# Moving one pair's query exponentials behind the next pair's copies, and loading the next block's activations two steps ahead

## The chip, the cores and the metric

The kernel runs on one core of one Trainium2 chip. The metric is the time on the device in microseconds (us), where lower is better. The profiler's trace of one execution gives what each engine did: TensorE (PE, with its weight loads as PEld), VectorE (DVE), ScalarE (ACT), GpSimd (POOL), and SyncE (SP), which issues most DMAs here.

## The reference

Two things stand one behind the other: attention with a random feature map in place of a softmax, for 8 batches of 8 heads, 576 positions and head size 64, and then a gated layer over its output as 4608 tokens of 512 channels.

```python
def phi(x):
    proj = np.einsum('bhsd,df->bhsf', x, w_phi)          # 64 -> 128 features
    proj = proj - np.max(np.abs(proj), axis=-1, keepdims=True)
    return np.concatenate([np.exp(proj), np.exp(-proj)], axis=-1)
q_p, k_p = phi(q), phi(k)
kv = np.einsum('bhsf,bhsd->bhfd', k_p, v)
z = np.sum(k_p, axis=2)
num = np.einsum('bhsf,bhfd->bhsd', q_p, kv)
den = np.einsum('bhsf,bhf->bhs', q_p, z)[..., None] + 1e-06
attn = num / den
x = attn.transpose(0, 2, 1, 3).reshape(B * S, H * D)      # 4608 x 512
out = (x @ w_a) * (x @ w_b) @ w_out                       # 512 -> 1536 -> 512
```

## The kernel before, in words

**Attention.** The heads are worked on in 32 pairs, named by batch and pair (3_1 is the second pair of batch 3; the trace leaves the numbers out). `attention_steps` writes a plan: each pair is given a period of four turns, and each part of its work (project, kv_products, num_products and so on) a turn counted from the start of its period. Parts of neighbouring pairs therefore interleave. `project` is the part that the change touches. TensorE projects the first half of q (pq), then k (pk), then the second half of q (pq), each into one of a few PSUM buffers. ScalarE copies the two halves of q out into p (L199 and L211), VectorE takes k's largest absolute value (m, L178) and subtracts it (d, L179), and ScalarE makes the two exponentials e of k (L181, L182). In every second pair the last 64 positions of two pairs' k, the rest, are treated in the same way as e_r. The features of q lie across the partitions, so for q the largest absolute value is a reduction over partitions on GpSimd (mb, L217, two per pair), VectorE subtracts it from p (L218) and ScalarE makes q's two exponentials eq (L219, L220). Then e and v are multiplied (kv), the sums are put beside them, back copies the result out (L263), it is transposed (pt), copied to kvh (L271), and multiplied with eq into the numerator (pn, copied to x at L284) and the denominator (pd, copied to dn at L295). The denominator goes through memory: stored as den, loaded as r, inverted, stored as rec, loaded for all partitions as rb, multiplied into x, and x is stored as xnorm.

**The gated layer, first pass.** The first half of the layer's 1536 columns is done in blocks of 384 tokens. Pairs 0 to 9 run alone, for some 117 us. From then on `run` gives TensorE parts of `moe_block` between the parts of a pair. A block loads x in four chunks of 128 channels (`x_chunk`, tile x32 with two buffers), splits each into a rounded high part xh and a low part xl (`x_make`: ScalarE casts, VectorE subtracts, L143 and L144), then goes through six steps f, each with the products pa and pb, their product h, and its parts hh and hl, and then through four output chunks po, each copied to o (L583, two buffers) and stored as part (L584). Chunks 0 and 1 of the next block are issued at f = 2. Chunks 2 and 3 are issued in the output loop, each behind the split that gives its x32 buffer free. The weights w come in a packed form, and `load_weights` decodes them beside the first 200 us: ScalarE at L421, VectorE at L422 and L424, ScalarE's cast at L427, VectorE at L429, L430 and L433.

**What comes behind.** From about 540 to 660 us the factors of the second pass are made from its weights on VectorE and ScalarE beside the last blocks. The second pass, from about 777 us on, does the other half of the columns. The change leaves both as they are.

**What sets the order.** On TensorE the order of the attention's products and the blocks' products is the order in which the plan issues them, held by explicit dependences (`pe`). On ScalarE, VectorE and SyncE a scheduler sorts the instructions by what they wait for; `tc.issue_after(x)` keeps an instruction behind x. Each engine runs its instructions in that order.

Of the kernel before, what the change touches and what calls it, by code (L numbers as in the profile page):

```python
# [9 lines left out]
F32 = mybir.dt.float32  # L10
# [8 lines left out]
P = 128  # L19
# [25 lines left out]
def tile_kernel(ctx, tc, qP, km, kr, vm, vr, w_phi, eye, w_a, w_b, w_out, out):  # L45
# [139 lines left out]
    def project(b, pr, a1, a2, consts, st):  # L185

        w2 = consts[0]
        u = f"{b}_{pr}"
        k32, q32 = st["k", b, pr], st["q", b, pr]
        p32 = a2.tile([P, 2, S], F32, tag="p32", name=f"p32_{u}")  # L190

        def q_half(t):
            x = duo(f"pq_{u}_{t}")
            for j in range(2):
                mm(x[:, j, :HALF], w2[heads[j]], q32[heads[j], times[t]])
            return x

        x = q_half(0)
        nc.scalar.copy(p32[:, :, times[0]], x[:, :, :HALF])  # L199
        y = duo(f"pk_{u}")  # L200
        for c in range(NFULL):
            for j in range(2):
                mm(y[:, j, c * P : (c + 1) * P], k32[heads[j], c * P : (c + 1) * P], w2[heads[j]])
        i = b * NPAIR + pr
        place = alone["early"] if i <= ALONE and i % 2 else a1
        st["e", b, pr] = features(u, y, NFULL, place, a1, a2)
        x = q_half(1)
        if pr % 2 == 0:
            for j in range(2):
                mm(x[:, j, HALF : HALF + F], st["rk", b, pr // 2][heads[j]], w2[heads[j]])  # L210
        nc.scalar.copy(p32[:, :, times[1]], x[:, :, :HALF])  # L211
        if pr % 2 == 0:
            st["er", b, pr // 2] = features(f"r_{u}", x[:, :, HALF:], 1, a1, a1, a2)
        eq = a1.tile([P, 2, 2, S], F32, tag="eq", bufs=2, name=f"eq_{u}")
        for j in range(2):
            mb = a2.tile([P, S], F32, tag="mb", name=f"mb_{u}_{j}")
            nc.gpsimd.partition_all_reduce(mb, p32[:, j], P, bass_isa.ReduceOp.absmax)  # L217
            nc.vector.tensor_tensor(p32[:, j], p32[:, j], mb, op=ALU.subtract)  # L218
        nc.scalar.activation(eq[:, :, 0], p32, AF.Exp)  # L219
        nc.scalar.activation(eq[:, :, 1], p32, AF.Exp, scale=-1.0)  # L220
        st["eq", b, pr] = eq

    def summed(b, pr, a1, a2, consts, st):

# [101 lines left out]
    def attention_steps(pools, consts, st):  # L326
# [11 lines left out]
        for i in range(B * NPAIR):  # L338
            b, pr = divmod(i, NPAIR)
            t0 = TURNS * i  # L340
            args = (b, pr, *pools, consts, st)
            at = SPREAD if i < ALONE else PACKED
            if i == ALONE - 1:
                at = dict(SPREAD, turned_kv=8, num_products=8, den_products=8)
            elif i == ALONE:
                at = dict(PACKED, kv_products=4, z_products=4, kv_out=4)
            units = ((project, 0), (turned_kv, 0), (summed, 0), (kv_products, 0), (num_products, 0), (z_products, 0), (kv_out, 0))
            units += ((den_products, 0), (load_kq, -5), (load_v, -2 if i else 0))
            for order, (f, t) in enumerate(units):
                if f is not summed or i >= SUM_FROM:  # L350
                    plan(order, once(f, *args), [t0 + at.get(f.__name__, t)])
            rec_turns = REC_TURNS0 if i < ALONE - 4 else REC_TURNS1 if i < ALONE - 2 else REC_TURNS
            done = t0 + at["den_products"]
            plan(10, reciprocals(b, pr, *pools, st), [done + t for t in rec_turns])
            if b == 0:
                plan(11, x_first, [done + rec_turns[-1] + t for t in X_TURNS])
            if pr == NPAIR - 1:
                plan(12, b, [done + rec_turns[-1]])
# [131 lines left out]
        key, i = two[q, nm, k]  # L490
        return weights[key][:, i]

    def x_chunk(p, j, c, pool, bufs):

        T, u = TS[p], f"{p}_{j}"
        x32 = pool.tile([P, T], F32, tag="x32", bufs=bufs, name=f"x32_{u}_{c}")
        t = j * T
        while t < (j + 1) * T:
            b, s0 = divmod(t, S)
# [5 lines left out]
    def x_make(p, j, c, x32, pool):  # L505
        hl = [pool.tile([P, TS[p]], F32R, tag=f"x{k}", bufs=NCC, name=f"x{k}_{p}_{j}_{c}") for k in "hl"]
        split(*hl, x32, nc.scalar, nc.vector)
        block_x.setdefault(j, []).append(hl)

    def first_block_x():  # L510

# [8 lines left out]
    def moe_block(p, j):  # L520
# [17 lines left out]
        for f in range(NFS[p]):  # L538
# [18 lines left out]
            hs.append((hh, hl))  # L557
            if f == 2 and j + 1 < blocks[0]:
                loaded = [x_chunk(p, j + 1, c, pool, 2) for c in range(2)]
            yield  # L560
        dst = part.rearrange("(c p) s -> p c s", p=P)[:, :, j * T : (j + 1) * T]
        accs = {}
# [10 lines left out]
        for cc in range(ahead):  # L573
            outputs(cc, range(NFS[p] - 1))
        for cc in range(NCC):
            if loaded:
                x_make(p, j + 1, cc, loaded.pop(0), pool)
                if cc + 2 < NCC:
                    loaded.append(x_chunk(p, j + 1, cc + 2, pool, 2))
            outputs(cc, range(NFS[p] - 1 if cc < ahead else 0, NFS[p]))  # L580
            acc = accs[cc]
            o = hpool.tile([P, T], F32, tag="o", bufs=2, name=f"o_{p}_{j}_{cc}")
# [288 lines left out]
        return wpool, f"w_{f}_{nm}"  # L871

    kept, begun, feeds = {}, set(), []
    weights, pools_moe, xpools, block_x, blocks, marks, acts, loads, alone = {}, [], [xpool], {}, [0], [], [], [], dict(turn=0)
    begin = TURNS * (ALONE + 1)
    with ExitStack() as c:
        pools = attention_pools(c)
# [163 lines left out]
```

## Time and profile before

| what | value |
|---|---|
| median of 3 runs | 1190.28 us (1188.46 to 1190.87) |
| time of the profiled execution | 1188.66 us |
| its span | 1186.9 us |
| TensorE busy | 1143.6 us, 96% |
| VectorE busy | 753.6 us, 63% |
| ScalarE busy | 566.4 us, 48% |
| GpSimd busy | 141.8 us, 12% |
| granted TensorE clock, mean | 0.996 of full speed |

The time of an execution is its span and some 1.8 us round it. Busy times are summed over an engine's instructions. The span has stages with different limits, so a share of 96% says how much idle time there is, not where it lies: the tables by window and the waits tell that.

### The profile page before, as it was taken

The page shows a single profiled execution, that of the slowest core. Times are in us where ns is not written, and L with a number is a line of the kernel's source. Part 1 is how long each engine was busy: PE and PEld are TensorE (multiplying, and loading weights), DVE is VectorE, ACT ScalarE, POOL GpSimd, SP SyncE. Part 2 cuts the span into 40 slices and gives each one's busy share as a digit, 9 for nine tenths or more (in the row PEclk, how much of TensorE's full clock was granted, in tenths as well). Part 3 has the DMA queues.
Part 4 walks back from the last instruction along what each step waited for, and adds up shares of the span by engine and source line. Part 5 has one row for each costly group of instructions (what it writes and reads, how often), then busy time and mean ns, then how long its engine had stood idle before and what let it go on. Part 6 is the DMA issues. An engine that isn't in the chain of part 4 may idle for free.

```text
span 1186.9 us, 21022 instructions
## 1 busy us (share of the span) xinstructions
PE 1143.6 (96%) x8198; PEld 1028.5 (87%) x8198; DVE 753.6 (63%) x1359; ACT 566.4 (48%) x1050; POOL 141.8 (12%) x69
## 2 busy tenths in 40 slices
PE   8998898999999999999999999999999999999998
PEld 5665775878788788889899999999999999999997
DVE  6897876554555455543899222648577685958665
ACT  6886565554454455442555222435344353535332
POOL 4443322212121121210000000000000000000000
PEclk9999998999999999999999999999999999999999
DMA  6576554323232333214885111067685777768572
GB/s 210 161 216 202 173 159 124 111 78 115 82 121 88 104 95 94 88 33 146 292 308 200 54 54 40 20 201 273 191 303 173 259 223 233 245 206 281 173 250 84
DMA packets 103077, 191.76 MB, mean 162 GB/s; under 512 B 19521, under 2 KB 54721, under 8 KB 102977
## 3 DMA queue, kind: packets, MB, share of 16 engines
q1 hardware_dynamic: 102672, 190.28, 50.2%
q8 instruction: 65, 1.06, 0.4%
q14 instruction: 36, 0.29, 0.1%
q10 hardware_dynamic: 304, 0.13, 0.0%
HBM read 150.75 MB, written 39.62 MB: 160 GB/s over the span
## 4 chain that ended last, share of the span: by engine, by line
PE 72%; DVE 12%; DMA 9%; ACT 4%; issue 2%; SPq 1%; ACTq 0%; DVEq 0%
PE po L105 10%; PE pa L105 10%; PE po L772 10%; PE pb L105 10%; PE pa L661 9%; PE pb L661 9%; PE kv L105 5%; PE pn L105 4%; DMA x<-xnorm 3%; PE pq L105 2%; PE pd L105 2%; DMA back_w<-kept_w 1%; PE pk L105 1%; DVE m L178 1%; DMA rb<-rec 1%
## 5 line engine op out<-in xcount | busy, mean ns | idle before, releaser
L217 POOL PARTITION_ALL_REDUCE mb<-p x64 | 141.5, 2255 | 371.4 <-ACT p L211 316.7
L105 PE MATMUL pa<-xh,w_a 128*128 128x384 f32 x576 | 161.4, 341 | 0.0
L105 PE MATMUL pb<-xh,w_b 128*128 128x384 f32 x576 | 158.6, 336 | 0.7 <-ACT o L583 0.7
L105 PE MATMUL po<-hh,w_o 128*128 128x384 f32 x576 | 155.4, 343 | 2.2 <-ACT o L583 2.2
L105 PEld LDWEIGHTS po<-hh,w_o 128*128 128x128 f32 x576 | 105.8, 190 | 8.1 <-ACT o L583 2.8
L105 PEld LDWEIGHTS pa<-xh,w_a 128*128 128x128 f32 x576 | 105.1, 188 | 5.5 <-ACT back L263 2.8
L105 PEld LDWEIGHTS pb<-xh,w_b 128*128 128x128 f32 x576 | 105.1, 188 | 1.0 <-ACT o L583 1.0
L553 DVE TENSOR_TENSOR h<-pb,h 128x384 f32<-128x384 f32 x72 | 39.8, 552 | 94.5 <-PE pb L105 89.9
L105 PE MATMUL po<-hl,w_o 128*128 128x384 f32 x288 | 97.5, 339 | 1.1 <-DVE hl L144 1.1
L105 PE MATMUL pb<-xl,w_b 128*128 128x384 f32 x288 | 96.8, 336 | 0.0
L105 PE MATMUL pa<-xl,w_a 128*128 128x384 f32 x288 | 96.7, 336 | 0.0
L178 DVE TENSOR_REDUCE m<-pk 128x8 f32<-128x1024 f32 x32 | 39.1, 1220 | 83.5 <-PE pk L105 83.5
L143 ACT CAST hh<-h 128x384 fp32r<-128x384 f32 x72 | 37.0, 514 | 95.8 <-DVE h L553 95.7
L772 PE MATMUL po<-hh_s,own_o 128*128 128x384 f32 x288 | 80.3, 336 | 0.3 <-ACT u L760 0.3
L105 PE MATMUL pn<-eq,kvh 128*64 128x288 f32 x512 | 68.0, 408 | 8.5 <-DVE kvh L271 8.2
L105 PEld LDWEIGHTS pn<-eq,kvh 128*64 128x64 f32 x512 | 37.6, 137 | 33.3 <-ACT p L211 4.3
L105 PE MATMUL kv<-e,v 128*64 128x256 f32 x512 | 62.3, 385 | 0.9 <-ACT e L182 0.9
L772 PE MATMUL po<-hh_w,own_o 128*128 128x384 f32 x216 | 59.1, 334 | 0.0
L105 PE MATMUL pq<-q,w 64*128 64x288 f32 x256 | 49.3, 452 | 9.7 <-ACT p L199 9.7
L105 PEld LDWEIGHTS po<-hl,w_o 128*128 128x128 f32 x288 | 54.7, 190 | 1.4 <-DVE hl L144 1.4
L583 ACT COPY o<-po 128x384 f32<-128x384 f32 x48 | 22.5, 478 | 69.6 <-PE po L105 57.3
L105 PEld LDWEIGHTS pa<-xl,w_a 128*128 128x128 f32 x288 | 54.2, 188 | 0.0
(257 smaller groups left out, 2619.7 us busy)
## 6 DMA issues: line engine op xcount, KB each, us to landing
back_s<-kept_s SPq DMA_DIRECT2D x71, 512.0 KB
back_w<-kept_w SPq DMA_DIRECT2D x52, 512.0 KB
q<-in_qP SPq DMA_DIRECT2D x32, 288.0 KB
rb<-rec SPq DMA_DIRECT2D x64, 144.0 KB
xnorm<-x SPq DMA_DIRECT2D x32, 288.0 KB
part<-o SPq DMA_DIRECT2D x48, 192.0 KB
o<-part SPq DMA_DIRECT2D x24, 384.0 KB
out_x<-o SPq DMA_DIRECT2D x48, 192.0 KB
```

Of the source, the lines that this page charges most:

```text
L105: issue = lambda: nc.tensor.matmul(out, w, x, start=start, stop=stop, skip_group_check=True)
L143: (eng_hi.copy if eng_hi is nc.scalar else eng_hi.tensor_copy)(hi, src)
L178: nc.vector.tensor_reduce(out=m, in_=p, op=ALU.max, axis=AX.X, apply_absolute_value=True)
L217: nc.gpsimd.partition_all_reduce(mb, p32[:, j], P, bass_isa.ReduceOp.absmax)
L553: nc.vector.tensor_tensor(h32, pab["b"], h32, op=ALU.mult)
L583: nc.scalar.copy(o, acc)
L661: in_turn(lambda: nc.tensor.matmul(acc[to][i], w_, x_, skip_group_check=True, **at), u.startswith("1_0"))
L772: in_turn(lambda: nc.tensor.matmul(acc[m, to], w_, h_, skip_group_check=True, **f), False)
```

## The change

Two things are moved. First, q's exponentials have a part of their own in the plan, `q_features`, one period (four turns) behind `project`, and are kept behind the latest copy of a second half of q, which is then that of the next pair. Second, a block loads chunks 2 and 3 of the next block's x at f = 3, into the two buffers of tile o, and splits them first, in front of the first output chunk; chunks 0 and 1, still loaded at f = 2, are split in front of the second. `block_x` becomes a dictionary so that the chunks are found by number.

```diff
-        nc.scalar.copy(p32[:, :, times[1]], x[:, :, :HALF])
+        copies.append(nc.scalar.copy(p32[:, :, times[1]], x[:, :, :HALF]))
...
-        eq = a1.tile([P, 2, 2, S], F32, tag="eq", bufs=2, name=f"eq_{u}")
         for j in range(2):
             mb = a2.tile([P, S], F32, tag="mb", name=f"mb_{u}_{j}")
             nc.gpsimd.partition_all_reduce(mb, p32[:, j], P, bass_isa.ReduceOp.absmax)
             nc.vector.tensor_tensor(p32[:, j], p32[:, j], mb, op=ALU.subtract)
-        nc.scalar.activation(eq[:, :, 0], p32, AF.Exp)
-        nc.scalar.activation(eq[:, :, 1], p32, AF.Exp, scale=-1.0)
-        st["eq", b, pr] = eq
+        st["p", b, pr] = p32
+
+    def q_features(b, pr, a1, a2, consts, st):
+        eq = st["eq", b, pr] = a1.tile([P, 2, 2, S], F32, tag="eq", bufs=2, name=f"eq_{b}_{pr}")
+        with tc.issue_after(copies[-1].ins):
+            nc.scalar.activation(eq[:, :, 0], st["p", b, pr], AF.Exp)
+            nc.scalar.activation(eq[:, :, 1], st["p", b, pr], AF.Exp, scale=-1.0)
...
-            units = ((project, 0), (turned_kv, 0), ...
+            units = ((project, 0), (q_features, TURNS), (turned_kv, 0), ...
...
             if f == 2 and j + 1 < blocks[0]:
                 loaded = [x_chunk(p, j + 1, c, pool, 2) for c in range(2)]
+            if f == 3 and loaded:
+                loaded += [x_chunk(p, j + 1, c, hpool, 2, "o") for c in range(2, NCC)]
...
         for cc in range(NCC):
-            if loaded:
-                x_make(p, j + 1, cc, loaded.pop(0), pool)
-                if cc + 2 < NCC:
-                    loaded.append(x_chunk(p, j + 1, cc + 2, pool, 2))
+            if loaded and cc < 2:
+                for c in (2, 3) if cc == 0 else (0, 1):
+                    x_make(p, j + 1, c, loaded[c], pool)
```

On ScalarE, beside block 0, where pair 3_1 is projected, the order was this; the number behind a name tells tiles apart, 3_1 is the pair in p, and in eq, e and dn only the pair within its batch is named.

```order
L421 ACTIVATE w_1_o<-raw_1_o 128x512
L219 ACTIVATE eq_0_1760<-p_3_0_1726 128x2x576
L220 ACTIVATE eq_0_1760<-p_3_0_1726 128x2x576
L263 COPY back_0_1882<-kv_0_1840 128x384
L427 CAST w_1_o<-w_1_o 128x512
L295 ACTIVATE dn_3_1893<-pd_3_1884,eps 128x288
L199 COPY p_3_1_1913<-pq_1_0_1914 128x2x288
L211 COPY p_3_1_1913<-pq_1_1_1934 128x2x288
L181 ACTIVATE e_1_1931<-d_1_1927 128x8x128
L182 ACTIVATE e_1_1931<-d_1_1927 128x8x128
```

The changed kernel has the same work there in this order (its lines are numbered 3 higher from L216 on).

```order
L424 ACTIVATE w_1_o<-raw_1_o 128x512
L266 COPY back_0_1879<-kv_0_1837 128x384
L430 CAST w_1_o<-w_1_o 128x512
L298 ACTIVATE dn_3_1890<-pd_3_1881,eps 128x288
L199 COPY p_3_1_1910<-pq_1_0_1911 128x2x288
L211 COPY p_3_1_1910<-pq_1_1_1931 128x2x288
L223 ACTIVATE eq_0_1941<-p_3_0_1723 128x2x576
L224 ACTIVATE eq_0_1941<-p_3_0_1723 128x2x576
L181 ACTIVATE e_1_1928<-d_1_1924 128x8x128
L182 ACTIVATE e_1_1928<-d_1_1924 128x8x128
```

The exponentials eq of pair 3_0 have moved from in front of the copies of pair 3_1 to behind them, and now stand between the copies and the exponentials e of 3_1's k; the cast and dn still stand ahead of the first copy.

On ScalarE at the end of block 0, where pair 3_3 is projected, the order was this; xh_1_0 to xh_1_3 are the high parts of the chunks of block 1's x, and x_3_1 is the attention's numerator.

```order
L143 CAST xh_1_2_2498<-x_0_1_2_2357 128x384
L284 COPY x_3_1_2244<-pn_1_2235 128x576
L219 ACTIVATE eq_2_2148<-p_3_2_2114 128x2x576
L220 ACTIVATE eq_2_2148<-p_3_2_2114 128x2x576
L143 CAST xh_1_3_2532<-x_0_1_3_2425 128x384
L263 COPY back_2_2266<-kv_2_2224 128x384
L421 ACTIVATE w_5_o<-raw_5_o 128x512
L295 ACTIVATE dn_1_2277<-pd_1_2268,eps 128x288
L199 COPY p_3_3_2290<-pq_3_0_2291 128x2x288
L427 CAST w_5_o<-w_5_o 128x512
```

In the changed kernel the same stretch, with two rows more at either end, reads as follows.

```order
L143 CAST xh_1_3_2360<-x_0_1_3_1989 128x384
...
L430 CAST w_4_o<-w_4_o 128x512
L287 COPY x_3_1_2247<-pn_1_2238 128x576
L266 COPY back_2_2269<-kv_2_2227 128x384
L424 ACTIVATE w_5_o<-raw_5_o 128x512
L298 ACTIVATE dn_1_2280<-pd_1_2271,eps 128x288
L199 COPY p_3_3_2293<-pq_3_0_2294 128x2x288
L430 CAST w_5_o<-w_5_o 128x512
L211 COPY p_3_3_2293<-pq_3_1_2314 128x2x288
L223 ACTIVATE eq_2_2324<-p_3_2_2117 128x2x576
L224 ACTIVATE eq_2_2324<-p_3_2_2117 128x2x576
```

All of xh has moved ahead of the cast of w_4_o, so between that cast and q's copy only x's copy, back, the first step of w_5_o and dn are left.

On SyncE the loads of chunks 2 and 3 of block 1's x stood here, among the stores and loads of the denominators (rec, rb, den); xnorm_84 and xnorm_85 are batches 0 and 1 of the normalised x.

```order
L314 DMA rec_79<-r_0_2160 128x9
L501 DMA x_0_1_2_2357<-xnorm_84 128x192
L318 DMA rb_0_2324<-rec_79 64x576 x2
L501 DMA x_0_1_2_2357<-xnorm_85 128x192
L169 DMA v_4_0_2373<-in_vm 128x512
L501 DMA x_0_1_3_2425<-xnorm_84 128x192
L501 DMA x_0_1_3_2425<-xnorm_85 128x192
```

In the changed kernel they stand some 50 rows sooner, beside the loads of chunk 1.

```order
L321 DMA rb_3_1580<-rec_77 64x576 x2
L504 DMA x_0_1_2_1986<-xnorm_84 128x192
L504 DMA x_0_1_2_1986<-xnorm_85 128x192
L504 DMA x_0_1_1_1826<-xnorm_84 128x192
L504 DMA x_0_1_1_1826<-xnorm_85 128x192
L504 DMA x_0_1_3_1989<-xnorm_84 128x192
```

The four loads have moved ahead of the raw weights and of two pairs' denominators; from the next block on, the loads of chunks 2 and 3 stand behind the stores of the o tiles whose buffers they take.

## Rows read from the trace of the kernel before

**Rows 1.** The page's first part: busy time, share of the span and instructions.

```profile
PE 1143.6 (96%) x8198; PEld 1028.5 (87%) x8198; DVE 753.6 (63%) x1359; ACT 566.4 (48%) x1050; POOL 141.8 (12%) x69
```

**Rows 2.** TensorE's waits, 60 to 117 us: line waited for, total, times, longest.

```profile
PE pn L105 <- DVE kvh L271: 4.3, 3, 1.9
PE pt L269 <- ACT dn L295: 1.9, 2, 1.0
```

**Rows 3.** TensorE's waits, 117 to 180 us.

```profile
PE pq L105 <- ACT p L199: 6.4, 3, 3.1
```

**Rows 4.** TensorE's timeline, 185 to 203 us: start, duration, instruction, idle before and releaser.

```profile
190.02 2.08 PE L105 MATMUL pk<-w,k 64*128 64x128 f32 x16 [2.96 <-ACT x L284]
194.40 1.33 PE L105 MATMUL pq<-q,w 64*128 64x288 f32 x4 [2.30 <-ACT p L199]
```

**Rows 5.** Windows: busy PE, PEld, DVE, ACT, POOL, then TensorE's clock, DMA share, GB/s.

```profile
190.00:200.00 10.00, 7.68 (x35) 6.62 (x36) 7.08 (x12) 7.51 (x11) 3.49 (x2) 0.50 0.42 122
570.00:630.00 60.00, 57.10 (x326) 56.14 (x326) 54.36 (x130) 34.83 (x84) 0.00 (x0) 1.00 0.87 295
```

**Rows 6.** TensorE's waits, 201.3 to 540 us.

```profile
PE pq L105 <- ACT p L199: 1.1, 5, 0.2
```

**Rows 7.** TensorE's waits, 570 to 630 us.

```profile
PE po L105 <- ACT o L583: 2.2, 2, 1.3
```

**Rows 8.** ScalarE's timeline, 136 to 159 us.

```profile
138.81 0.64 ACT L421 ACTIVATE w_b<-raw_b 128x512 f32<-128x512 f32 x1
...
152.74 1.17 ACT L219 ACTIVATE eq<-p 128x1152 f32<-128x1152 f32 x1
...
154.86 0.46 ACT L263 COPY back<-kv 128x384 f32<-128x384 f32 x1
...
156.14 0.64 ACT L199 COPY p<-pq 128x576 f32<-128x576 f32 x1
```

**Rows 9.** TensorE's timeline, 137 to 164 us.

```profile
141.01 0.39 PE L105 MATMUL pq<-w,rk 64*128 64x128 f32 x4
...
145.97 1.30 PE L105 MATMUL kv<-e,v 128*64 128x256 f32 x10
...
156.83 0.76 PE L105 MATMUL pq<-q,w 64*128 64x288 f32 x4 [2.77 <-ACT p L199]
```

**Rows 10.** ScalarE's timeline, 178 to 202 us.

```profile
179.35 0.42 ACT L181 ACTIVATE e_r<-d_r 128x256 f32<-128x256 f32 x1
...
188.92 0.51 ACT L143 CAST xh<-x 128x384 fp32r<-128x384 f32 x1 [5.57 <-DMA x<-xnorm]
...
192.76 0.67 ACT L421 ACTIVATE w_o<-raw_o 128x512 f32<-128x512 f32 x1
...
193.70 0.65 ACT L199 COPY p<-pq 128x576 f32<-128x576 f32 x1
...
197.91 1.06 ACT L181 ACTIVATE e<-d 128x1024 f32<-128x1024 f32 x1 [1.49 <-DVE d L179]
```

**Rows 11.** VectorE's timeline, 60 to 203 us, four instructions.

```profile
73.24 1.78 DVE L433 TENSOR_TENSOR w_a<-w_a 128x512 fp32r<-128x512 f32 x1
...
136.51 0.68 DVE L433 TENSOR_TENSOR w_a<-w_a 128x512 fp32r<-128x512 f32 x1
...
185.88 0.68 DVE L433 TENSOR_TENSOR w_o<-w_o 128x512 fp32r<-128x512 f32 x1
...
196.60 1.22 DVE L179 TENSOR_TENSOR d<-pk,m 128x1024 f32<-128x1024 f32 x1
```

**Rows 12.** GpSimd's timeline, 60 to 203 us, two of its pairs of all-reduces.

```profile
72.66 5.01 POOL L217 PARTITION_ALL_REDUCE mb<-p  x2 [5.74 <-DVE kvh L271]
...
196.51 4.29 POOL L217 PARTITION_ALL_REDUCE mb<-p  x2 [16.19 <-ACT p L211]
```

**Rows 13.** TensorE's timeline, 206 to 222 us.

```profile
212.30 0.39 PE L105 MATMUL pq<-w,rk 64*128 64x128 f32 x4
...
219.39 1.95 PE L105 MATMUL kv<-e,v 128*64 128x256 f32 x16
```

More of the change, by code (lines that the diff above doesn't have):

```diff
@@ L346, in attention_steps @@
                 at = dict(PACKED, kv_products=4, z_products=4, kv_out=4)
-            units = ((project, 0), (turned_kv, 0), (summed, 0), (kv_products, 0), (num_products, 0), (z_products, 0), (kv_out, 0))
+            units = ((project, 0), (q_features, TURNS), (turned_kv, 0), (summed, 0), (kv_products, 0), (num_products, 0), (z_products, 0), (kv_out, 0))
             units += ((den_products, 0), (load_kq, -5), (load_v, -2 if i else 0))
@@ L491, in weight, with x_chunk @@
         return weights[key][:, i]
-    def x_chunk(p, j, c, pool, bufs):
+    def x_chunk(p, j, c, pool, bufs, tag="x32"):
         T, u = TS[p], f"{p}_{j}"
-        x32 = pool.tile([P, T], F32, tag="x32", bufs=bufs, name=f"x32_{u}_{c}")
+        x32 = pool.tile([P, T], F32, tag=tag, bufs=bufs, name=f"x32_{u}_{c}")
         t = j * T
@@ L507, in x_make @@
         split(*hl, x32, nc.scalar, nc.vector)
-        block_x.setdefault(j, []).append(hl)
+        block_x.setdefault(j, {})[c] = hl
     def first_block_x():
@@ L873, in tile_kernel @@
     kept, begun, feeds = {}, set(), []
-    weights, pools_moe, xpools, block_x, blocks, marks, acts, loads, alone = {}, [], [xpool], {}, [0], [], [], [], dict(turn=0)
+    weights, pools_moe, xpools, block_x, blocks, marks, acts, copies, loads, alone = {}, [], [xpool], {}, [0], [], [], [], [], dict(turn=0)
     begin = TURNS * (ALONE + 1)
```

## The prediction

> **What bounds the kernel now.** I read the page's first part, then the table of the windows by stage, then TensorE's waits stretch by stage, and last the timelines round the longest of them. The first part says that TensorE is busy for 1143.6 of 1186.9 us [rows 1]. So a change that leaves the matmuls alone can only win back what TensorE stands idle, or what it does at the lower clock. The change touches nothing behind the first pass, so the idle time of the last stage, from 777 us on, stays. What is left are the waits ahead of that, and there are few. Between 60 and 117 us, before the blocks run beside the attention, TensorE waits for kvh on VectorE and for dn on ScalarE, 6.2 us in all [rows 2]. Between 117 and 180 us it waits three times for the copy of q's projection, 6.4 us [rows 3]. Round 190 us, at the end of block 0, it waits twice, 2.96 us for x's copy and 2.30 us for q's copy, and then runs for some 10 us at a granted clock of 0.50, which is 1.2 of 2.4 GHz [rows 4, 5]. With 7.68 us of work in that window, the lower clock costs half of it, 3.84 us. From 201 to 540 us the copy of q costs 1.1 us in five waits [rows 6], and the stretch from 570 to 630 us, where the factors of the second pass are made beside the last blocks, leaves 60 - 57.1 = 2.9 us idle, 2.2 of it behind copies of o [rows 5, 7].
>
> **Why these waits are there.** Round 154 us the chain can be read directly. TensorE is done with pk, but pq's second half has to wait until ScalarE has copied the first half out; the copy starts at 156.14 us, behind the two exponentials of the pair before, which started at 152.74 us and let the next instruction go at 154.86, and behind back, a cast and dn [rows 8]. TensorE resumes at 156.83 us [rows 9]. At 190 us the chain is longer: ScalarE stands for 5.57 us on xh, whose load of x came late because chunk 2 had to wait for a free x32 buffer; behind it stand x's copy, the exponentials, dn and q's copy [rows 10].
>
> **The change, part by part.** No matmul, exponential, copy or reduction is added or taken away. Two exponentials per pair move, and two chunks of x per block are loaded sooner. On SP two issues fewer is nothing.
>
> *Pairs 12 and 13 (q waits at 140 and 157 us).* At 157 us the two exponentials stand in front of the copy for 154.86 - 152.74 = 2.12 us [rows 8], and VectorE's part of the cast between is ready, so the copy comes 2.1 us sooner, at 154.0, and its end, 154.7, is still what TensorE waits for: 2.1 of the 2.77 us come back. At 140 us the weight decode takes over: the next weight's first step starts at 138.81 us today, and could start when VectorE is done with the last weight's low part, at 136.51 + 0.68 = 137.19 [rows 8, 11]; but the cast now stands ahead of the copy as well. The step and dn take 0.94 us together, from 192.76 to 193.70 [rows 10], and the cast (taken like the step) and the copy 0.64 each [rows 8], so the copy ends at about 139.5, and TensorE can go on 0.9 us sooner than at 140.4, where it resumes now, half a microsecond ahead of 141.01 [rows 9]. Together 3.0; the bounds are 0 (the decode eats all) and 6.4 (every wait goes).
>
> *The end of block 0.* All four chunks are loaded before they are wanted, so xh no longer holds up ScalarE and the first wait, 2.96 us, goes. What takes its place: VectorE now makes two more low parts before it finishes the weight, so its end moves from 185.88 + 0.68 = 186.56 to about 187.7 us (two of 0.56); then w, dn and q's copy, some 1.6 us, give 189.3 against a TensorE that could go on at about 187.9: 1.4 us late. And behind pq ScalarE now runs a burst before kv may start: copy 0.64, exponentials 2.1, e's 2.0, so 4.7 to 4.9 us [rows 8, 10]. The gap on TensorE between pq and kv here was 5.6 us, 2.1 of which was the low clock, so 3.5 at full clock; with 1.1 us for the late VectorE kv waits some 2.5 us. Of 2.96 + 2.30 + 3.84 = 9.1 us, 9.1 - 1.4 - 2.5 = 5.2 come back. Upper bound 9.1. If the two waits that are left pull the clock down again, it is 5.2 - 3.84 = 1.4, the lower bound.
> The row that speaks of the clock is the one at 190 us: 2.96 us of waiting, then 0.50 granted [rows 4, 5]. The Trainium skill's page TensorE: Matmul & The Clock Gate, Part 1, says that the gate opens with activity and closes with idling; the trace agrees with its two levels. That speaks against this term: if the 1.4 us of waiting that I leave close the gate again, it gives 1.4 us, as in its lower bound, and the sum would be 9.5.
>
> *Alone, 60 to 117 us.* Here VectorE is what TensorE waits for. GpSimd's all-reduce starts when the second half of q is copied (72.66 us, two for 5.01 us together), and runs until 77.7 us beside VectorE's decode of the weights [rows 12]. The low part of a weight took 1.78 us in that time and 0.68 us in another; d, which reads PSUM, took 1.22 us in full overlap with GpSimd at 196.60 us [rows 11, 12]. The copy now goes ahead of the exponentials, GpSimd starts about 2.1 us sooner, and its overlap moves from the decode to m, d and kvh. That gives VectorE some 1 us per pair, five pairs in this stretch, about 5 of the 6.2 us at most. Half of the 6.2, 3 us, is what I take, as the rest can be lost to dn and to loads; bounds -1 (a later e costs kv once) and 6.2.
> The Trainium skill's GPSIMD Engine Reference, section Key points, says that GpSimd shares its SBUF interfaces with VectorE and disturbs instructions with two SBUF inputs; the 1.78 us row is such an instruction, and by the page alone the term would be nearer 5 than 3.
>
> *From 201 to 540 us.* The five small waits for q's copy, 1.1 us, go: +1.1 [rows 6]; bounds 0 and 1.1.
>
> *The three short gaps.* With the burst of 4.9 us behind pq, kv waits where the blocks put little between pq and kv. Three pairs have 4.57 us there (as from 141.40, the end of pq, to 145.97), one is the 5.6 us above, the other 17 of the 21 pairs have from 6.70 (212.69 to 219.39) to 13 us [rows 9, 13]. Price: 3 x 0.33 = 1.0 us, so -1.0; bounds -3.4 (0.8 us more in each of the three, if the pair brings the two short exponentials of the rest, 0.42 us each [rows 10]) and 0.
>
> *From 570 to 630 us.* x's chunks for the next block no longer queue in ScalarE's way in the output loop, so o's copies come in time: +2.0 of 2.2 [rows 7]; bounds 0 and 2.9. The new loads cost nothing as they lie two steps ahead of their use; if a store of o held their buffers too long, it would be the old wait again.
>
> Sum: 3.0 + 5.2 + 3.0 + 1.1 - 1.0 + 2.0 = 13.3 us. The profiled execution took 1188.66 us, so 1175.4. It lies 1.6 us under the median of the runs, 1190.28, so the changed kernel's median should be about **1177 us**. The sum of the upper bounds is 25.7 (1165), of the lower ones -3.0 (1193); with terms off in different directions the forecast's own range is 1171 to 1184.
>
> **The rivals.**
> 1. *The decode takes the place of the exponentials.* ScalarE's order keeps casts that wait for VectorE ahead of q's copy; if they come late, the terms at 140 and 157 us give nothing and the end of block 0 only 1.4, the alone stage 1. With 2.0 and 1.1 - 1.0 that is 4.5 us: 1186. For it: the 1.78 us that a decode step can take beside GpSimd [rows 11]; against: at 157 us nothing of it waits today.
> 2. *All of the idle time goes.* GpSimd's shift frees VectorE fully and the clock never falls: 6.2 + 6.4 + 9.1 + 1.1 + 2.2 - 1.0 = 24, less what dn keeps, over 20: about 1168.
> 3. *Slower: the burst ends after kv is due in most pairs.* Place: behind pq in every pair beside blocks. It decides when the burst ends more than 7.7 us after pq: then the three shortest gaps cost 9.4, the next 2.1, the four at 6.7 us 4.0, 15.8 with one at 7.4, more than the 13 gained. At 8 us it is about 19 us, and the time 1177 + 19 - 1 = 1195. For it: the e's now stand behind two exponentials in every pair. Against: 5.7 us, with 0.8 for the rest's exponentials, still ends inside 6.7 [rows 13].
> 4. *The loads don't come sooner.* If chunks 2 and 3 wait for o's stores, or k, q and v come late behind r on SP's queue, the wait at 190 us stays and a microsecond goes in several early pairs: 1188 to 1190.
>
> **How the numbers follow.** The forecast has 0.60, rival 1 0.17, rival 2 0.10, rival 3 0.09, rival 4 0.04. A measurement can tell 0.2% from no change, 2.4 us, so faster means below 1187.9. The forecast is faster in nearly all its range (0.59), rival 1 in two thirds (0.11), rival 2 always (0.10): 0.80. Rival 3 gives slower 0.07 and rival 4 0.01: 0.08; what is left is the same, 0.12. The range of 1169 to 1189 leaves out half of rival 2, most of rival 3 and the tails of the forecast, some 0.17.
>
> **What would show it.** Right: TensorE's waits for q's copy between 117 and 201 us fall from 8.7 to about 4 us or less; ScalarE does not wait for x's load at 189 us; the window round 190 us is back above 0.9 of the clock; GpSimd's pairs start behind d or sooner in the alone stage, and VectorE's 1.78 us steps become rarer; kv waits for e a few times, for 0.3 us each, and once for 2 to 3. Wrong: a new wait of pq for a copy behind a cast; kv's waits for e over 1 us in many pairs; the clock at 0.5 after another wait; SP's loads of x behind the stores of o.

## The result and the profile after

The changed kernel took 1198.95 us (median of 6 runs, 1194.69 to 1201.62) against 1189.78 us before; the ratio of the means is 1.0072, with a 95% interval of 1.0049 to 1.0096. A second series beside other kernels gave 1.0071 (1.0043 to 1.0099). By the ratio it is 8.6 us slower, where 13 us faster was forecast, and the time lies outside the range.

The profiled execution has a span of 1197.3 us, against 1186.9. The page's first part of the changed kernel, and then its windows (busy time of PE, PEld, DVE, ACT and POOL, TensorE's clock, DMA share, GB/s):

```profile
PE 1149.8 (96%) x8198; PEld 1029.5 (86%) x8198; DVE 744.6 (62%) x1359; ACT 562.4 (47%) x1050; POOL 140.7 (12%) x69
```

```profile
60.00:117.00 57.00, 47.59 (x596) 30.79 (x594) 44.22 (x68) 41.56 (x63) 21.80 (x10) 0.94 0.64 197
...
190.00:200.00 10.00, 8.67 (x107) 6.55 (x103) 9.16 (x15) 6.30 (x10) 3.23 (x2) 1.00 0.50 152
200.00:210.00 10.00, 7.64 (x64) 4.44 (x65) 4.94 (x8) 3.89 (x6) 1.03 (x1) 0.83 0.35 120
570.00:640.00 70.00, 68.22 (x386) 66.19 (x385) 64.48 (x154) 39.48 (x96) 0.00 (x0) 1.00 0.86 284
```

The window at 190 us, which stood at a clock of 0.50 before [rows 5], is at 1.00. But from 60 to 117 us TensorE is idle for 9.4 us, and it does what work there is at 0.94 of the clock. Busy time has grown by 6.2 us with the same 8198 matmuls: part of that is work done at the lower level, where the rest comes from was not followed. TensorE's waits of the changed kernel (line waited for, total, times, longest), in the stretches 60:117, 117:180, 180:215, 215:548 and 570:640:

```profile
PE pn L105 <- DVE kvh L274: 7.4, 3, 6.8
PE pt L272 <- ACT dn L298: 2.0, 2, 1.4
...
PE pq L105 <- ACT p L199: 4.3, 3, 3.1
PE pa L105 <- DVE kvh L274: 0.7, 1, 0.7
...
PE kv L105 <- ACT e L182: 2.8, 1, 2.8
PE pq L105 <- ACT p L199: 0.9, 1, 0.9
...
PE pa L105 <- DVE kvh L274: 3.3, 5, 0.7
PE po L105 <- DVE hl L144: 2.0, 1, 2.0
PE pq L105 <- ACT p L199: 1.1, 5, 0.2
...
PE pb L105 <- ACT o L587: 1.1, 2, 0.8
PE po L105 <- ACT o L587: 0.5, 1, 0.5
```

Against [rows 2, 3, 4, 6, 7]: the waits for q's copy and for x at the end of block 0 have shrunk; a single wait of 6.8 us for kvh is new, and so are six of 0.65 us of pa for kvh. A wait says little of what is won or lost in sum, so I compare the start of the transposes (pt, one per pair) in the two traces; a row of the table is that start minus the one before the change, in us. Each column is one traced execution, and not each lies near the median of its runs: r's order took 1198.35 us here (median 1193.68), the exponentials alone 1190.99 (1194.12). The fastest two are the versions named below "the low parts of x behind hl" and "the exponentials late for the alone pairs only".

| pair | change | change, second trace | r's order alone | exponentials alone | x alone | both, old order | fastest two: first | second |
|---|---|---|---|---|---|---|---|---|
| 1 | 1.4 | 1.1 | 1.5 | -0.6 | 1.0 | 1.4 | 0.2 | 0.4 |
| 7 | -0.2 | -1.3 | 1.8 | -2.3 | 1.0 | -1.3 | -2.3 | -1.7 |
| 9 | 7.5 | 3.6 | 8.4 | 1.0 | 1.7 | 2.1 | -2.6 | -2.4 |
| 10 | 8.0 | 3.1 | 8.2 | 0.7 | 1.8 | 2.6 | 0.4 | 0.2 |
| 13 | 6.2 | 1.2 | 11.1 | -0.5 | 2.1 | 0.7 | -0.9 | 0.5 |
| 14 | 0.3 | -4.7 | 10.9 | -1.1 | -2.3 | -5.2 | -4.6 | -3.6 |
| 24 | 4.6 | -0.1 | 10.0 | 1.3 | -2.2 | -2.2 | -0.8 | -3.2 |
| 31 | 8.2 | 3.4 | 10.0 | 3.9 | 0.5 | 1.3 | -1.8 | -4.2 |

The column of the change has four parts: a gain of 1.6 us from pair 1 to 7, a loss of 7.7 to pair 9, a gain of 7.7 from pair 10 to 14, and then a slow loss of 7.9 up to pair 31. The prediction has the two gains. The losses are what had to be explained.

**The loss at pair 9.** Two rows of VectorE's timeline of the kernel before, and then VectorE's and TensorE's timelines of the changed kernel (the first row of VectorE's there and the last two of TensorE's are used further down):

```profile
97.98 0.76 DVE L321 TENSOR_TENSOR x<-x,rb 128x576 f32<-128x576 f32 x1 [0.42 <-DMA rb<-rec]
...
102.45 0.55 DVE L271 COPY kvh<-pt 128x384 f32<-128x384 f32 x1
```

```profile
74.44 0.68 DVE L436 TENSOR_TENSOR w_a<-w_a 128x512 fp32r<-128x512 f32 x1
...
96.11 0.76 DVE L324 TENSOR_TENSOR x<-x,rb 128x576 f32<-128x576 f32 x1 [3.45 <-DMA rb<-rec]
100.50 0.76 DVE L324 TENSOR_TENSOR x<-x,rb 128x576 f32<-128x576 f32 x1 [3.64 <-DMA rb<-rec]
...
102.45 0.75 DVE L217 TENSOR_TENSOR p<-p,mb 128x576 f32<-128x576 f32 x1
...
108.35 0.55 DVE L274 COPY kvh<-pt 128x384 f32<-128x384 f32 x1
```

```profile
109.04 1.23 PE L105 MATMUL pn<-eq,kvh 128*64 128x288 f32 x4 [6.81 <-DVE kvh L274]
...
202.36 1.97 PE L105 MATMUL kv<-e,v 128*64 128x256 f32 x8 [2.76 <-ACT e L182]
...
233.89 0.49 PE L272 MATMUL pt<-ident,back 128*128 128x128 f32 x3
235.03 0.45 PE L105 MATMUL pa<-xh,w_a 128*128 128x384 f32 x1 [0.65 <-DVE kvh L274]
```

VectorE stands for 3.45 and 3.64 us on the product of x with rb, a row that comes by DMA (before, 0.42 us on the second of the two and nothing on the first); behind it, in order, stand q's subtraction, m, d and kvh. Twice is the point to see: not one instruction stands badly, the DMA chain itself is late. SyncE's waits up to 117 us, of the kernel before and then of the change, and SyncE's timeline in both (each time den's store, what is issued behind it, and the rec and rb of the second product):

```profile
SPq L318 <- DMA rec<-r: 3.1, 3, 2.6
SPq L310 <- DMA den<-dn: 2.3, 2, 1.3
```

```profile
SPq L321 <- DMA rec<-r: 15.4, 8, 3.2
SPq L313 <- DMA den<-dn: 12.6, 7, 3.3
```

```profile
78.39 0.52 SPq L307 DMA_DIRECT2D den<-dn  x1
78.95 0.44 SPq L153 DMA_DIRECT2D k<-in_km  x1
79.49 0.38 SPq L155 DMA_DIRECT2D q<-in_qP  x1
...
83.60 0.38 SPq L310 DMA_DIRECT2D r<-den  x1
...
88.07 0.54 SPq L314 DMA_DIRECT2D rec<-r  x1
...
92.56 0.47 SPq L318 DMA_DIRECT2D rb<-rec  x1
```

```profile
82.27 0.52 SPq L310 DMA_DIRECT2D den<-dn  x1
84.59 0.32 SPq L313 DMA_DIRECT2D r<-den  x1
84.97 0.42 SPq L153 DMA_DIRECT2D k<-in_km  x1
...
92.30 0.54 SPq L317 DMA_DIRECT2D rec<-r  x1
...
96.21 1.09 SPq L321 DMA_DIRECT2D rb<-rec  x2
```

Before, r's load was issued 5 us behind den's store, with k, q, rk, v and rec between. Now it stands directly behind it, and SyncE waits 1.8 us for the store to be complete; in the same way rb waits for rec. In these two kinds of wait that is 22.6 us more. SyncE does not wait that much longer in all: all its waits up to 117 us add up to some 61 us before and 65 us in the change, as others have shrunk. What has changed is where the queue stands still, and with it when each step of the chain is issued: rb leaves at 96.21 us where it left at 92.56, and that of the product ahead of it is 4.2 us late. The diff names no such move. It comes from `enumerate(units)`: the added part moves load_v from place 9 to place 10, and place 10 is that of the reciprocal chain; within one turn the older pair's chain now goes ahead of the load of v, and `behind(loads, ...)` then ties r to an earlier load.

The Trainium skill, DMA: Bandwidth & Descriptors, Anatomy of one DMA, puts the fixed cost of a transfer, described there for those that GpSimd issues, at about 2 us, most of it the confirmation that the last byte has landed. The 1.8 us from the end of den's issue (82.79) to r's (84.59), both SyncE's, are near it.

**The slow loss beside the blocks.** The last two rows of TensorE's timeline above are one of six such places: pa waits 0.65 us for kvh, which it does not use. It waits for the PSUM buffer in which pt lay, which kvh's copy gives free. With what comes with the wait each place costs 0.9 us from one pair's pt to the next. In the kernel before, pa followed pt without a wait.

### The profile page after: what moved, and what is told of

It reads as the page before. It is cut to its first block, busy times and chain, and to the rows that moved or that the text cites. A ratio compares the mean times of both kernels' runs of the same rounds, so it can differ in the third digit from the quotient of the medians.

```text
span 1197.3 us, 20998 instructions
## 1 busy us (share of the span) xinstructions
PE 1149.8 (96%) x8198; PEld 1029.5 (86%) x8198; DVE 744.6 (62%) x1359; ACT 562.4 (47%) x1050; POOL 140.7 (12%) x69
## 4 chain that ended last, share of the span: by engine, by line
PE 73%; DMA 11%; DVE 10%; ACT 3%; issue 2%; SPq 1%; ACTq 0%; DVEq 0%
PE pa L105 10%; PE pb L105 10%; PE po L105 10%; PE po L776 9%; PE pa L665 9%; PE pb L665 9%; PE kv L105 6%; PE pn L105 5%; PE pq L105 3%; DMA x<-xnorm 2%; PE pd L105 2%; DMA back_w<-kept_w 2%; DMA rec<-r 2%; PE pk L105 1%; DMA rb<-rec 1%
## 5 line engine op out<-in xcount | busy, mean ns | idle before, releaser
L216 POOL PARTITION_ALL_REDUCE mb<-p x64 | 140.4, 2235 | 379.9 <-ACT p L211 355.0
L105 PE MATMUL pn<-eq,kvh 128*64 128x288 f32 x512 | 71.2, 422 | 11.2 <-DVE kvh L274 11.2
L555 ACT COPY h<-pa 128x384 f32<-128x384 f32 x72 | 34.3, 477 | 55.2 <-PE pa L105 53.7
L105 PEld LDWEIGHTS kv<-e,v 128*64 128x64 f32 x512 | 34.5, 139 | 25.5 <-issue 7.2
```

The costliest lines, as they stand in the source:

```text
L105: issue = lambda: nc.tensor.matmul(out, w, x, start=start, stop=stop, skip_group_check=True)
L555: nc.scalar.copy(h32, pab["a"])
```

## The experiments

Each is the kernel before or the changed kernel with the edit shown; the lines of the two parts of the change are as in its diff. Lines that only keep a handle to an instruction are left out, and so are the plan numbers behind the chain's, which are raised with it.

**The order of r alone.**

```diff
-            plan(10, reciprocals(b, pr, *pools, st), [done + t for t in rec_turns])
+            plan(9, reciprocals(b, pr, *pools, st), [done + t for t in rec_turns])
```

> The kernel before, with one number changed: in the plan of a turn the reciprocal chain gets the same place as the load of v (9 instead of 10), as the added part did unseen in the change, so that r's load stands directly behind den's store on SyncE. Theory A (this order is what lost 7 us at pair 9, since r waits there for den's store while k, q, v and rb stand behind it): slower than before by 4 to 8 us, 1194 to 1198, with VectorE waiting for rb round 100 us. Theory B (the late exponentials lose it, as VectorE's order puts decode steps and q's subtractions ahead of kvh): no difference from before, 1188.5 to 1191.

Measured 1.0036 (1.0017 to 1.0054), 4.3 us slower. Theory A holds, at the low end of what it named; in the table most of the loss stands at pair 9, as in the change.

**The exponentials alone**, with the chain's number raised to 11, so that the chain keeps its place.

```diff
+            units = ((project, 0), (q_features, TURNS), (turned_kv, 0), ...
-            plan(10, reciprocals(b, pr, *pools, st), [done + t for t in rec_turns])
+            plan(11, reciprocals(b, pr, *pools, st), [done + t for t in rec_turns])
```

> Only q's exponentials a period later, with the reciprocal chain in its old place and x loaded as before. Theory A: faster than before by 2 to 6 us, 1184 to 1188, since the waits for q's copy at 140 and 157 us shrink and the alone stage does not lose. Theory B: slower by 4 to 9 us, 1194 to 1199, with the loss in the alone stage and six waits of 0.65 us for kvh beside the blocks.

Measured 1.0042 (1.0024 to 1.0059), 5.0 us slower. So theory B holds beside theory A: either move alone loses. In the table the alone stage gains 1.7 us up to pair 7, then loses 3.2 by pair 9, where TensorE's transposes wait 4.8 us for dn (two experiments further down this wait is taken up), and the six places beside the blocks take the rest.

**x's loads alone.**

```diff
+            if f == 3 and loaded:
+                loaded += [x_chunk(p, j + 1, c, hpool, 2, "o") for c in range(2, NCC)]
```

> Only x's chunks two steps ahead, half of them in the outputs' buffers; q's exponentials and the reciprocal chain as before. Both theories: the load no longer holds up ScalarE at 189 us, so 3 to 6 us faster than before, 1184 to 1187; if the splits ahead of the last hidden parts cost what they save, 1189 to 1191. A rival C, that this part is what made the change slow (loads behind the stores of o): 1193 or more.

Measured 1.0007 (0.9990 to 1.0024): no difference. The 4.4 us come at pair 14, as both theories had it, but 2.6 of them go again between pairs 24 and 31, where four splits stand ahead of hl: TensorE waits 2.0 us for hl there, against 1.1 before, and its granted clock is 0.86 from 398 to 410 us, against 1.00. Rival C falls: the loads behind the stores of o cost nothing that shows.

**Both moves, with the chain in its old place** (the change with number 11 for the chain).

> The changed kernel with the reciprocal chain put back behind the load of v in the plan of a turn; q's exponentials late and x early as in the change. Theory A: what was predicted of the change comes out, 1177 to 1185. Theory B: it stays slower than before, 1194 to 1200, with TensorE's wait for kvh of several us near 109 us.

Measured 1.0027 (1.0007 to 1.0047), 3.2 us slower: r's order is about half of the loss, not all, and neither theory's number comes out. The rows of this version at 110 us, VectorE, ScalarE and TensorE, show a second, independent loss:

```profile
108.25 0.76 DVE L324 TENSOR_TENSOR x<-x,rb 128x576 f32<-128x576 f32 x1 [4.66 <-DMA rb<-rec]
108.93 0.42 DVE L425 TENSOR_SCALAR w_b<-w_b 128x512 uint32<-128x512 uint32 x1
```

```profile
109.38 0.62 ACT L430 CAST w_b<-w_b 128x512 fp32r<-128x512 f32 x1 [3.86 <-DVE w_b L425]
109.90 0.49 ACT L298 ACTIVATE dn<-pd,eps 128x288 f32<-128x288 f32 x1
```

```profile
110.45 0.90 PE L272 MATMUL pt<-ident,back 128*128 128x128 f32 x3 [4.69 <-ACT dn L298]
```

A weight's first shift on VectorE has come to stand behind the product that waits for rb; ScalarE's cast waits for the shift, dn stands behind the cast, and TensorE's transposes wait for dn. Before, the shift stood one place ahead of the product.

**That shift in its old place**: the version above, with one instruction moved by one place. (In versions with this edit the lines behind it are numbered one higher.)

```diff
+        what = [shifts["0_3_b"]] if (b, pr) == (1, 2) else marks
-        behind(marks, lambda: nc.vector.tensor_tensor(x32, x32, rb, op=ALU.mult))
+        behind(what, lambda: nc.vector.tensor_tensor(x32, x32, rb, op=ALU.mult))
```

> Late exponentials and early x with the reciprocal chain in its old place, and one instruction of VectorE moved by one place: the first shift of the weight w_3_b stands again ahead of the product of x of pair 1_2 with rb, which waits for a DMA. Theory D (with the late exponentials the scheduler put that shift behind the product, so that the cast, dn and TensorE's transposes at 110 us wait for rb): the 4.7 us wait of pt for dn goes, and the time falls by 3.5 to 5 us against the version without it (1193.3), to 1188 to 1190. Rival (rb is late anyway, and whatever stands behind it waits): 1192 to 1194.

Measured 0.9996 (0.9974 to 1.0018), 3.7 us less than without it, as theory D had it, though the two intervals overlap. The traces agree: pt of pair 9 starts 2.3 us sooner than before the change, and 2.1 us later without this edit. Its rows, VectorE and TensorE:

```profile
103.81 0.43 DVE L426 TENSOR_SCALAR w_b<-w_b 128x512 uint32<-128x512 uint32 x1 [0.68 <-ACT w_b L425]
107.14 0.76 DVE L325 TENSOR_TENSOR x<-x,rb 128x576 f32<-128x576 f32 x1 [2.90 <-DMA rb<-rec]
```

```profile
106.06 0.55 PE L272 MATMUL pt<-ident,back 128*128 128x128 f32 x3 [0.93 <-ACT dn L298]
```

The wait for rb is still there, 2.9 us of it, but nothing that TensorE needs stands behind it: 4.69 us have become 0.93.

**The exponentials behind e**, beside the blocks only; the chain is in its old place, the shift is not.

```diff
-        with tc.issue_after(copies[-1].ins):
+        with tc.issue_after((copies if b * NPAIR + pr < ALONE else acts)[-1].ins):
```

> Late exponentials and early x with the reciprocal chain in its old place, but beside the blocks q's exponentials stand behind the next pair's e instead of in front of it. Theory H (the waits of 0.65 us for which the profile names kvh are waits for h's copy of pa, which stands behind ScalarE's burst): that copy comes 1 to 1.5 us later still where the pair is odd, so these five or six waits grow to 1.5 to 2.2 us each; the wait of kv for e near 201 us shrinks from 2.8 to under 1 us; in all 1194 to 1200. Rival K (kvh itself is late): the waits stay at 0.65 us each, and with kv's wait gone 1190 to 1192.

Measured 1.0041 (1.0020 to 1.0062), at 1196.35 us. That is inside theory H's range, but by luck: kv's wait near 201 us is gone, and 4.2 us of waiting for a weight, which no theory had, took its place there. The mechanism of theory H falls on three rows, TensorE's, VectorE's and ScalarE's:

```profile
230.17 0.45 PE L105 MATMUL pa<-xh,w_a 128*128 128x384 f32 x1 [1.11 <-DVE kvh L274]
```

```profile
229.57 0.54 DVE L274 COPY kvh<-pt 128x384 f32<-128x384 f32 x1
```

```profile
230.30 0.46 ACT L555 COPY h<-pa 128x384 f32<-128x384 f32 x1
```

pa starts right behind kvh and ahead of h's copy, so it does not wait for that copy. The wait grew to 1.11 us because kvh itself now stands behind another instruction of VectorE. Theory K has it right that kvh is waited for, but not its time, and not why pa waits for it: the programs say on which engine's semaphore pa waits, here for the same matmul in the kernel before and in the change, with its row before.

```
549 L105 MATMUL pa_1_1_2693<-xh_1_0_2353,w_1_a 128x384 [waits Activation_49]
547 L105 MATMUL pa_1_1_2690<-xh_1_0_2425,w_1_a 128x384 [waits DVE_49]
```

```profile
231.66 0.44 PE L105 MATMUL pa<-xh,w_a 128*128 128x384 f32 x1
```

Three PSUM buffers are handed out where the program is built. Before, this pa took the buffer that ScalarE's copy of h gives free; in the change it takes pt's.

**The exponentials behind the block's copy of h**, with the shift in its old place.

```diff
-            units = ((project, 0), (q_features, TURNS), ...
+            units = ((project, 0), (q_features, TURNS if i < ALONE else TURNS + 1), ...
-        with tc.issue_after(copies[-1].ins):
+        with tc.issue_after((hcopies or copies)[-1].ins):
```

> The version with the shift of w_3_b in its old place, and beside the blocks q's exponentials a turn later still, behind the copy h of the block's next step. Theory H: the waits of 0.65 us go (0.9 us each with what comes with them), kv no longer waits for e near 201 us: 5 to 8 us less than without it, 1181 to 1185. Rival K: the waits of 0.65 us stay, 1186 to 1188.

Measured 0.9970 (0.9950 to 0.9991), 3.6 us faster than before and the first version that is faster at all. It took 4.0 us less than the version without this edit (1186.88 and 1190.91), less than the 5 to 8 of theory H, and the intervals overlap; the waits of 0.65 us are gone, all six. The same pa waits on ScalarE's semaphore again, and its row has no wait; kvh runs only at 228.48 us.

```profile
227.26 0.45 PE L105 MATMUL pa<-xh,w_a 128*128 128x384 f32 x1
```

So what the change did here is settled: with ScalarE's burst ahead of h's copy pa got another buffer, and the buffer brought the wait. That the builder's planned time of h's copy is what it chose by is argued from this, not shown.

**The low parts of x behind hl**, on top of that.

```diff
-                    x_make(p, j + 1, c, loaded[c], pool)
+                    with tc.issue_after(hs_low.ins):
+                        x_make(p, j + 1, c, loaded[c], pool)
```

> As the version with the exponentials behind h's copy, and the low parts of the next block's x kept behind the last low part of h (hl). If the wait of po for hl near 405 us (2.0 us in the change, 1.05 before) comes from the four splits that stand ahead of hl, it goes here: 1 to 3 us less, 1179 to 1184. Rival (hl waits for h's product anyway): no difference.

Measured 0.9950 (0.9927 to 0.9973), 6.0 us faster than before. Against the version without this edit that is 2.4 us, as much as was named, but the intervals overlap, and the time, 1185.87 us, is above the range. What is sure is the wait: TensorE's wait for hl near 400 us falls from 1.99 to 0.2 us, and VectorE's order shows why:

```profile
399.61 0.55 DVE L144 TENSOR_TENSOR hl<-h,hh 128x384 fp32r<-128x384 f32 x1
400.08 1.95 DVE L144 TENSOR_TENSOR xl<-x,xh 128x384 fp32r<-128x384 f32 x4
```

**The exponentials late for the alone pairs only**, on top of that; beside the blocks they stand as before the change.

```diff
-            units = ((project, 0), (q_features, TURNS if i < ALONE else TURNS + 1), ...
+            units = ((project, 0), (q_features, TURNS if i < ALONE else 0), ...
-        with tc.issue_after((hcopies or copies)[-1].ins):
+        with tc.issue_after(copies[-1].ins) if b * NPAIR + pr < ALONE else nullcontext():
```

> The fastest version so far, but q's exponentials late only for the pairs that run alone; beside the blocks they stand as before. If late exponentials pay beside the blocks once nothing waits behind them (q's copy at 140 and 157 us): 1.5 to 4 us slower than the fastest, 1187 to 1190. Rival (only the alone stage and the loads of x pay): no slower, 1184 to 1187.

Measured 0.9956 (0.9939 to 0.9974), 5.2 us faster, the same as the version before within the intervals. So the rival's time comes out: behind h's copy, late exponentials beside the blocks pay nothing that shows. They don't shorten what they were moved for there: from 117 to 550 us TensorE's waits for q's copy are 10.0 us in the version before and 9.7 in this one. In the change, where the exponentials stand directly behind that copy, they are 6.3 us, and the six waits of pa are the price; a place that has the one without the other was not tried. The rival's other half, that the alone stage pays, is not shown either. In the table's last two columns the gain of pair 7 is used up by pair 10: TensorE waits 2.7 and 2.2 us for kvh there, and its granted clock is 0.72 from 110 to 116 us in both, 1.00 before the change.

**r's order in the fastest version**, and then **the product moved behind q's subtraction** in that.

```diff
-            plan(11, reciprocals(b, pr, *pools, st), [done + t for t in rec_turns])
+            plan(10, reciprocals(b, pr, *pools, st), [done + t for t in rec_turns])
```

```diff
-        what = [shifts["0_3_b"]] if (b, pr) == (1, 2) else marks
+        what = [shifts["0_3_b"]] if (b, pr) == (1, 2) else [shifts[2, 1]] if (b, pr) == (1, 1) else marks
```

The fastest version is that with the low parts of x behind hl.

> The fastest version so far with r's load directly behind den's store, as in the change. Theory A (this order costs by itself): 3 to 7 us slower, 1189 to 1193, with VectorE waiting for rb at the product of x of pair 1_1 near 97 to 101 us. Rival (it costs only together with the late exponentials in front of kv, or the loss in the change was the clock's): within 1 us of the fastest.

> As the version with r's load directly behind den's store, and the product of x of pair 1_1 with rb moved on VectorE by some five places, behind the second subtraction of q. If the loss comes from what stands behind that product (q's subtraction, then GpSimd, m, d and kvh): 2 to 6 us come back, 1185 to 1188. Rival (it comes from SyncE, whose loads of k, q and v start later): no change, 1189 to 1193.

Measured 1.0037 (1.0015 to 1.0058) and 1.0034 (1.0012 to 1.0057). The order of r costs 10 us against the fastest version (0.9950, in another series), more than theory A named, and moving the product gives nothing back: VectorE then stands at the next instruction of the chain, the reciprocal of r.

```profile
101.12 0.22 DVE L315 RECIPROCAL r<-r 128x9 f32<-128x9 f32 x1 [4.33 <-DMA r<-den]
```

So it is not the place of this one product: the whole chain is late, and the next of its instructions takes over the wait, still ahead of q's subtraction. The rival's time comes out, but what it named, the later loads of k, q and v, is not shown to cost anything: from 60 to 117 us TensorE waits for kvh (6.7 us) and dn (3.9), and for no load.

**The change once more.**

> The changed kernel once more, beside the others on one chip, for a second trace. Slower than before by 5 to 11 us; if the places of the loss are those of the first trace, VectorE waits again for rb near 100 us with q's subtraction behind it, TensorE waits 5 us or more for kvh, and the five waits of 0.65 us stand again in blocks beside the attention.

Measured 1.0071, 8.4 us slower, as said. VectorE waits for rb again (1.74 and 3.08 us), TensorE for kvh for 4.54 us, a little under the 5 named, and the waits of 0.65 us are back, six of them. The size at pair 9 differs between the two traces, 7.7 and 4.9 us; the wait is shorter in the second, and the granted clock from 60 to 117 us is 0.97 there and 0.94 in the first.

## Why the prediction was wrong, step by step

**The step that failed** is the one sentence on SyncE: "On SP two issues fewer is nothing". The traces list the same number of issues in both kernels. What moved on SyncE was the order of the reciprocal chain, and it is worth 4.3 us alone, 5.4 us in the change (1.0072 with it, 1.0027 without) and 10 us in the fastest version. Rival 4 came near it, with k, q and v late behind r, priced it at a microsecond in several early pairs and gave it 0.04. It looked at the loads; what ends the wait is the chain den, r, rec, rb, whose every step is delayed by the wait for the step before, and VectorE's order, in which the path of TensorE stands behind rb. This step is the largest, not the only one: with the chain in its old place the two moves still lose 3.2 us. The other steps are below: a decode step sorted behind rb's product, pa's buffer, and x's splits ahead of hl. None of them had a term in the sum.

**Pairs 12 and 13**: 3.0 predicted; the starts of pt give 0.8 from pair 10 to 11 and 2.0 to pair 12, 2.8 in all (2.9 in the second trace). Right in size. At 157 us the wait for q's copy falls from 2.77 to 0.58 us, as worked out. At 140 us it falls further than worked out in the first trace, from 3.06 to 0.72, but the granted clock is 0.97 from 117 to 180 us there; in the second, at 1.00, it falls to 2.06. By pair 13 the first wait of pa takes 1.0 back.

**The end of block 0**: 5.2 predicted. From pair 13 to 14 5.9 us come back, and 2.1 go again by pair 15: 3.8. pq waits 0.92 us where 1.4 was worked out, kv 2.76 where 2.5 was, and ScalarE waits there for d on VectorE, as said. The difference is the clock, which fell behind kv's wait (0.83 from 200 to 210 us): between the forecast and its lower bound.

**Alone, 60 to 117 us**: +3.0 predicted. The mechanism is there, and gave 1.6 and 2.4 us by pair 7 in the two traces. GpSimd starts at 70.33 us instead of 72.66, and the weight's low part that took 1.78 us [rows 11] takes 0.68 at 74.44 us, as GpSimd is almost done by then. GpSimd's timeline (L216 and L217 of the changed kernel are L217 and L218 of the one before):

```profile
70.33 4.26 POOL L216 PARTITION_ALL_REDUCE mb<-p  x2 [4.73 <-ACT p L211]
```

The bound of -1 was wrong: it asked what a later e costs, not what else comes into another order. Two things did: r's order on SyncE, by the plan's numbers, and, under it, the shift behind the product, by the scheduler (3.7 us where r's order is the old one). From pair 7 to 9 the first alone loses 6.6 us and the version with the second alone 3.4, but the change 7.7, so the two don't add up there; the transposes that waited 4.69 us for dn wait 0.62 us in the change, where kvh is late already.

**From 201 to 540 us**: +1.1 predicted, 0 measured; the five waits for q's copy stand as they did, 1.1 us in five.

**The three short gaps**: -1.0 predicted; kv does not wait there. In its place came six waits of pa, 0.9 us each, -5.5. It is rival 3's burst, but what comes behind it is h's copy, and the price is paid through the PSUM buffer that pa is given. Rival 3 looked at when a result is ready, not at when a buffer comes free and to whom it goes.

**x's splits ahead of hl** had no term: -1.6 in the change by pair 25, -2.6 with x's loads alone, where the clock fell behind the wait.

**From 570 to 630 us**: +2.0 predicted; TensorE's idle time there falls from 2.9 to 1.8 us, so +1.1.

**Rival 1** came in one place. At 132 us pq waits 3.06 us for q's copy, where 0.53 us stood before at 124 us:

```profile
131.92 0.76 PE L105 MATMUL pq<-q,w 64*128 64x288 f32 x4 [3.06 <-ACT p L199]
```

VectorE stands there for 6.91 us on r's load, the decode stands behind it, and the copy behind the decode. It is the late chain again. Rival 2 did not come.

Left open: from pair 31 to the end the changed kernel loses another 2.2 us (1.3 in the second trace), though 1.1 come back in that stretch. In the first trace the second pass waits 4.9 us for its weights, against 3.2 before, in the second only 1.0. The traces of the other versions differ from the kernel before by -1.9 to +3.7 us there, without an edit to it, so this may be no effect of the change. And the fastest version was not run without any late exponentials: x's early loads with their splits behind hl could be all that it gains, since the 2.1 us by pair 7 (from pair 1 to 7, 0.4 to -1.7) are read from a trace alone and are gone by pair 10.

## What to carry to other kernels

Where a scheduler sorts an engine's queue, compare the order of every queue, SyncE's first, before and after a change, and ask of each instruction that waits for a DMA what now stands behind it; here one added entry in an enumerated list put a load directly behind the store that it reads, and cost 4.3 us alone and 10 us in the fastest version. Price a moved instruction by the buffers that it gives free late as well as by its result, since the builder may hand the next user another buffer. Work moved out of the way is still in the way of something: beside the blocks late exponentials either brought pa's waits or did not shorten the waits for q's copy, and the early loads showed no gain as long as their splits stood ahead of what TensorE waits for.

## What the runs showed of the hardware

The same wait was followed by full clock in one trace and by the lower level in another: near 23 us TensorE waits 2.64 us for kvh before pn, which then takes 2.16 us in the kernel before; in the change it waits 2.66 us and pn takes 3.57 us. The granted clock from 24 to 27 us is 1.00 in the first and 0.53 in the second. This is the 1.2 us by which several columns of the table start. It hardly comes from the edits: x's loads alone, whose edit is to the blocks, start by 1.0 as well. The runs of one kernel spread by 7 us (the change: 1194.69 to 1201.62), and with twelve runs the intervals still reach some 2 us to either side.
